# Adding a row shift on VectorE instead of TensorE, and loading the kept token rows in place

## The chip, the cores and the metric

The kernel runs on one core of one Trainium2 chip. A core has five engines that work side by side: TensorE (PE; its weight loads are PEld), VectorE (DVE), ScalarE (ACT), GpSimd (POOL) and SyncE (SP), which here only issues DMAs. The metric is the device time of one launch in microseconds (us). The profile is one execution recorded by the hardware profiler.

## The reference: what is computed

One block with adaptive layer norm: a long convolution (S4 form), then a bilinear GLU, on one sequence of 2048 tokens with 640 features, all in float32.

```python
mod = silu(c) @ w_mod                      # six vectors of 640: sa, ca, ga, sb, cb, gb
h = layernorm(x) * (1 + ca) + sa
# K[d, l] = Re sum_n C[d,n] * exp(dt*A[d,n]*l) * dt*B[d,n],  N = 192
x = x + ga * (causal_conv(h, K) + h * Dskip)
h = layernorm(x) * (1 + cb) + sb
x = x + gb * (((h @ w_gate) * (h @ w_up)) @ w_down)
```

## The kernel before, in words

The program has two halves. The first makes the convolution and writes the new rows x to `x2d` in HBM; the second is the GLU, nearly all matmuls. The features are cut into five column groups of 128 (`db`), the rows into four blocks of 4 x 128 (`q` or `c`).

The first half runs a loop of 120 steps (L1354): 40 units n of three steps each. In them ScalarE makes sines and cosines (`trig`), GpSimd the exponentials (`outer`), VectorE their products (`PtA`, `QtA`, `PtB`, `QtB`: L784, L785, L790, L810) and TensorE sums them to the convolution's kernel (`kg`: L825, L840). Between these, other units are placed by hand: every unit is a generator whose pieces have due numbers in the table `SCHED`, and `due` (L1289) runs the pieces of a step in order of their numbers. A step has 20 numbers; the loop over n ends at 2400, the first half at 2880. Every engine works its instructions in exactly that order, and so does the DMA queue of SP. Which of two or three buffers a unit takes is written out in the strings of `SLOT`.

The units that matter here:

- `u_pre(db, q)`, 20 of them: loads four blocks of normalised rows (L874) and makes the first stage of a transform over the rows: four 64 x 64 matmuls (L886, tile positions in the four quarters of the array), two into each of two PSUM banks `r[0]` and `r[1]`. The shift `sa` is the same for all rows of a column, and so its transform is a constant pattern times a row: four matmuls with a contraction of one row (`t_one` by `shr`) add it. ScalarE copies both banks out (`act`, L235 is the helper's line) and SP stores them to `FH` (L894, L897). For `db` = 0 GpSimd scales the rows first (L878).
- `u_k`, `u_g`, `u_c`: transform of the kernel, second stage of the rows (L907), product of the two (L946 to L956) and the first inverse stage (L967), whose result `W` is stored to `WD` (L972). For the last column group `u_c` works in two parts of 64 columns. The last four `W` stores alternate between two tiles, Wb and Wa.
- `u_d(db, c)`: loads a part of `WD` (`Vt`, L980) and the input rows (`xs`, L982, a ring of two tiles), makes the last inverse stage (L988), adds the input rows (L995) and stores the sum to `x2d` (L996). For the last two column groups and c = 0 or 1 the sum goes into the tile `XB[c]` instead (L992) and is stored from there, since the second half starts with these token rows. The other three column groups of `XB` are loaded back from `x2d` (`rows`, L1384).
- `u_head`: statistics of the rows in `XB` (L1156), the second layer norm, transposes (L1186) and the first GLU matmuls (L1223). While it waits, `warm` (L1196) runs matmuls whose result isn't used.

`need` checks in Python that a unit is placed behind those that it depends on; the waits in the program come from the tile framework. From step 121 on no kernel generation is left. `XB` is made there, in memory that the generation used before.

Of the kernel before, what the change touches and what calls it, by code (L numbers as in the profile page):

```python
# [10 lines left out]
F32 = mybir.dt.float32  # L11
# [7 lines left out]
P = 128  # L19
# [12 lines left out]
    ml=(47, -888, -934),  # L32
    mr=(((138, 140), (110, 111)), ((2, 74), (4, 83)), ((0, 27), (-862, 18))),
    st=(
        (48, 91),
        (69, 100),
        (71, 101),
        (-948, 5),
        (-1006, 0),
        (-965, 89),  # L40
        (-1010, -969),
        (-868, 34),
        (-938, -874),
        (-918, 0),
        (-1003, -929),
        (-947, -909),
        (-919, -868),
        (34, 63),
        (37, 69),
        (-912, 0),  # L50
    ),
    hm=(
        (10, 220),
        (302, 416),
        (-1002, 172),
        (-999, 389),
        (-1010, 182),
        (-961, 147),
        (59, 100),
        (123, 173),  # L60
        (246, 310),
        (290, 372),
        (162, 252),
        (121, 180),
        (210, 293),
        (297, 381),
        (391, 486),
        (473, 556),
    ),
    rstd=(124, 87),  # L70
    tab=(367, 828),
    fo=(162, 162, 208, 238),
    e0=(4, 158),
    ds=(483, 468, 275, 262),
    mc=((87, 192, 194, 200, 210), (153, 286, 303, 326, 337), (270, 359, 369)),
    q=(
# [4 lines left out]
    ),  # L81
    pre=(
# [5 lines left out]
    ),  # L88
    c=(
# [4 lines left out]
        (  # L94
            (2433, 2608, 2608, 2648, 2679, 2703),
            (2425, 2484, 2537, 2554, 2645, 2677),
            (2477, 2493, 2636, 2656, 2680, 2719),
            (2387, 2439, 2532, 2545, 2620, 2633),
# [8 lines left out]
    ),  # L107
    k=(
        (392, 464),
        (371, 384),  # L110
        (474, 512),
        (494, 503),
        (622, 637),
        (592, 599),
        (710, 710),
        (607, 639),
        (640, 677),
        (652, 660),
        (831, 865),
        (797, 803),  # L120
        (973, 990),
        (941, 961),
        (1060, 1060),
        (1060, 1060),
        (1125, 1152),
        (1353, 1363),
        (1274, 1275),
        (1390, 1425),
        (1482, 1495),
        (1506, 1519),  # L130
        (1576, 1590),
        (1524, 1542),
        (1757, 1758),
        (1791, 1791),
        (1747, 1747),
        (1720, 1720),
        (2005, 2019),
        (1893, 1909),
        (2048, 2049),
        (2020, 2031),  # L140
        (2083, 2095),
        (2218, 2252),
        (2287, 2298),
        (2350, 2355),
        (2328, 2328),
        (2344, 2352),
        (2461, 2497),
        (2497, 2510),
    ),
    low=(168, 419, 677, 899, 1101, 1385, 1631, 1857, 2075),  # L150
    w=(2478, 2613, 2684, 2668, 2879, 2879),
    wl=(2590, 2441),
    wm=(2732, 2755),
    h=(2709, 2738, 2775, 2811, 2843, 2843, 2857, 2875),
    g=(
# [1736 lines left out]
```

## Time and profile before

| | us |
|---|---|
| median of three runs | 965.52 |
| lowest and highest | 962.56, 967.35 |
| the profiled execution | 962.34 |
| its span, first to last instruction | 960.6 |
| TensorE busy | 892.6 |
| VectorE busy | 705.6 |
| ScalarE busy | 580.5 |
| GpSimd busy | 471.2 |
| first half, until about | 500 |

The granted TensorE clock is 0.989 on average. A row of the instruction views has start, length in us (or count and lengths in ns), engine, line, operation, output and inputs with shapes; a bracket at its end gives how long the engine idled before it and what ended that. In a group row, `x6 | 3.5, 590` is count, busy us in all, mean ns of one. SPq and ACTq are the queues' DMA issues; what lands later isn't in their length. Busy matmul records overlap, so a full PE isn't a PE at its peak.

### The profile page before, as it was taken

How to read it: one execution, taken by the hardware profiler on the slowest of the kernel's cores; microseconds unless marked ns; L12 is line 12 of the kernel's file. 1: busy time of each engine (PE TensorE's matmuls, PEld its weight loads, DVE VectorE, ACT ScalarE, POOL GpSimd, SP SyncE). 2: the span in 40 equal slices, each digit the busy share in tenths (PEclk: the TensorE clock that was granted, in tenths of full speed). 3: DMA queues.
4: the chain of work that ended last, by engine and by line, in shares of the span. 5: the costliest groups of instructions: out<-in, count | busy, mean ns of one | idle time of the engine just before them, and what ended most of it. 6: DMA issues, size and time to landing. Idle time of an engine off the chain costs nothing.

```text
span 960.6 us, 27559 instructions
## 1 busy us (share of the span) xinstructions
PE 892.6 (93%) x11646; PEld 734.0 (76%) x11646; DVE 705.6 (73%) x1250; ACT 580.5 (60%) x1016; POOL 471.2 (49%) x369
## 2 busy tenths in 40 slices
PE   1898787999899899998889999999999999999998
PEld 1675555878776677887558888889999788888997
DVE  8977888878888986767688555557585766569952
ACT  6989999887988977763276333234463543435430
POOL 3998997986699668750041345320013323231110
PEclk9989999999999999999999999999999999999999
DMA  7876546435267646547894675435536576758875
GB/s 238 324 243 242 186 131 199 146 108 153 78 207 197 187 124 194 184 128 228 277 308 152 192 246 192 165 140 172 200 120 196 171 238 208 244 172 289 253 231 189
DMA packets 158819, 188.59 MB, mean 196 GB/s; under 512 B 9828, under 2 KB 128360, under 8 KB 157544
## 3 DMA queue, kind: packets, MB, share of 16 engines
q1 hardware_dynamic: 149480, 155.51, 50.3%
q0 software_dynamic: 4752, 21.63, 7.8%
q10 hardware_dynamic: 4464, 9.70, 2.7%
q8 instruction: 91, 1.49, 0.6%
q14 instruction: 32, 0.26, 0.1%
HBM read 124.22 MB, written 62.59 MB: 194 GB/s over the span
## 4 chain that ended last, share of the span: by engine, by line
PE 61%; ACT 12%; issue 10%; DVE 7%; POOL 5%; DMA 4%; SPq 0%; POOLq 0%; DVEq 0%; ACTq 0%
PE pa L1095 19%; PE psg L1095 9%; PE pa L1527 7%; PE kg L825 3%; PE kg L840 2%; PE psfa L907 2%; PE psfb L967 2%; PE psfb L907 2%; ACT L235 2%; PE psfc L967 1%; PE psfc L907 1%; PE psfa L967 1%; PE psfc L886 1%; ACT trb L235 1%; ACT tra L235 1%
## 5 line engine op out<-in xcount | busy, mean ns | idle before, releaser
L1072 POOL TENSOR_TENSOR tf<-wur,wgb 128x256 f32<-128x256 f32 x23 | 17.5, 760 | 241.5 <-DVE wtl L1043 193.2
L729 POOL TENSOR_TENSOR EQ<-LQ,RH 128x1536 f32<-128x1536 f32 x40 | 114.8, 2870 | 5.3 <-DVE QtB L785 5.3
L1043 DVE TENSOR_TENSOR wtl<-tf,wth 128x256 fp32r<-128x256 f32 (+1 forms) x72 | 37.0, 516 | 59.2 <-ACT wth L235 59.2
L729 POOL TENSOR_TENSOR Phb<-LH,DH 128x1536 int32<-128x1536 int32 x21 | 60.3, 2871 | 32.6 <-ACT trb L235 19.3
L729 POOL TENSOR_TENSOR EP<-LP,RH 128x768 f32<-128x768 f32 x40 | 61.9, 1547 | 1.7 <-ACT RH L235 1.7
L729 POOL TENSOR_TENSOR Pha<-LH,DH 128x1536 int32<-128x1536 int32 (+1 forms) x20 | 54.1, 2703 | 9.2 <-ACT trb L235 8.5
L1527 PE MATMUL pa<-wsg,sh 128*128 128x384 f32 (+1 forms) x304 | 58.1, 309 | 0.0
L840 PEld LDWEIGHTS kg<-QtB,PtB 64*32 64x32 f32 x2560 | 38.3, 108 | 13.4 <-issue 6.9
L1043 DVE TENSOR_TENSOR wsg<-wga,wsg 128x640 fp32r<-128x640 f32 x36 | 35.5, 988 | 14.8 <-ACT wsg L235 14.8
L840 PE MATMUL kg<-QtB,PtB 64*32 64x64 f32 x2560 | 44.6, 219 | 1.8 <-DVE QtB L785 1.8
L1527 PEld LDWEIGHTS pa<-wsg,sh 128*128 128x128 f32 x304 | 45.4, 188 | 0.0
L1566 POOL DMA_DIRECT2D wsg<-wdc x21 | 11.2, 532 | 66.6 <-PE pa L1579 35.7
L235 ACT ACTIVATE sh<-a 128x512 fp32r<-128x512 f32 x55 | 33.3, 626 | 13.9 <-PE psg L1579 6.2
L1043 DVE TENSOR_TENSOR sl<-a,sh 128x512 fp32r<-128x512 f32 x55 | 38.0, 710 | 3.9 <-ACT sh L235 3.9
L235 ACT ACTIVATE wsg<-wga 128x640 fp32r<-128x640 f32 x36 | 26.2, 731 | 23.7 <-PE pa L1527 12.6
L1095 PE MATMUL pa<-hh,wsg 128*128 128x512 f32 x150 | 40.0, 393 | 0.0
L235 ACT ACTIVATE a<-pa 128x512 f32<-128x512 f32 x12 | 7.2, 596 | 49.9 <-PE pa L1095 49.9
L235 ACT ACTIVATE s<-pa 128x512 f32<-128x512 f32 x12 | 7.2, 598 | 49.2 <-PE pa L1095 47.0
L235 ACT ACT_TABLE_LOAD x25 | 32.1, 1283 | 7.2 <-DMA pta<-A_A_re 4.2
L784 DVE TENSOR_TENSOR QtA<-trb,EQ 128x1024 f32<-128x1024 f32 x22 | 26.8, 1216 | 11.9 <-POOL EQ L729 4.4
L235 ACT ACTIVATE wth<-tf 128x256 fp32r<-128x256 f32 (+1 forms) x72 | 32.4, 481 | 4.5 <-DVE tf L1073 1.8
L1527 PE MATMUL pa<-wsg,sl 128*128 128x384 f32 (+1 forms) x152 | 34.5, 308 | 0.0
(672 smaller groups left out, 3230.0 us busy)
## 6 DMA issues: line engine op xcount, KB each, us to landing
wsg<-wdc POOLq DMA_DIRECT2D x21, 640.0 KB, 5.1
wgb<-B_w_gate SPq DMA_DIRECT2D x24, 320.0 KB, 4.1
wur<-B_w_up SPq DMA_DIRECT2D x24, 320.0 KB, 5.6
wsd<-wsg SPq DMA_DIRECT2D x12, 640.0 KB, 3.7
wga<-wdg SPq DMA_DIRECT2D x12, 640.0 KB, 3.9
wsg<-wsd POOLq DMA_DIRECT2D x12, 640.0 KB, 4.8
wdc<-xb SPq DMA_DIRECT2D x21, 320.0 KB, 4.5
TVb<-WD SPq DMA_DIRECT2D x26, 256.0 KB, 3.5
```

Source lines behind the costliest of these rows:

```text
L235: return S.activation(o, i, f, **kw)
L729: G.tensor_tensor(o.rearrange("p x (h l) -> p x h l", l=8), lo.unsqueeze(2).to_broadcast([P, rows, nh, 8]), hi.unsqueeze(3).to_broadcast([ ...
L784: return [lambda: V.tensor_tensor(Qt[:, :, :, 0:32], tr[:, :, :, ::-1], e[:, :, 0:32].unsqueeze(1).to_broadcast([P, 2, R, 32]), op=OP.mult ...
L825: PE.matmul(kg[j * 32 : j * 32 + 32, dd, :], PtA[:, c, dl * 4 + j, :], QtA[:, c, dl * 4 + j, :], start=dd == 0 and c == 0, stop=False, til ...
L840: PE.matmul(kg[j * 32 : j * 32 + 32, dd, :], PtB[lo : lo + 64, c, r, :], QtB[lo : lo + 64, c, r, :], start=False, stop=dd == 7 and c == 1, ...
L907: PE.matmul(r[c][par * 64 : par * 64 + 64, i, :], t_tw[:, k0 + k, c, :], src[:, k, :], start=True, stop=True, tile_position=(0, par * 64))
L967: PE.matmul(r[par][:, i], t_ti[lo : lo + 64, qd * 4 + i, c, :], y[lo : lo + 64, i, :], start=k == 0, stop=k == len(x) - 1, tile_position=( ...
L1043: V.tensor_tensor(lo, v, hi, op=OP.subtract)
L1072: E.tensor_tensor(t[:, 0:2], u[:, 0:2], g[:, 0:2], op=OP.subtract)
L1095: PE.matmul(ps, w[a][:, k], x[b][:, l], start=first and n == 0 and m == 0, stop=n == 2 and m == len(ks) - 1, skip_group_check=True)
L1527: PE.matmul(AC[tb][t][c], x[:, ts], w[:, cs], start=st, stop=f == NF - 1 and n == 2 and (c == 0 or t % 2 == 1))
L1566: G.dma_start(WD[q], wdc[:, q // 3, q % 3])
```

## The change

There are three edits, and an order that was written anew:

1. In `u_pre` the one-row matmuls are left for bank 1 only. Bank 0's shift is added as VectorE takes that bank out of PSUM: `scalar_tensor_tensor` with the shift row (spread over the partitions in `shr`), a column of constants `t_on`, and `r[0]`. Bank 1 is still copied by ScalarE. The table `t_c` shrinks from 800 to 737 columns accordingly.
2. In `u_d`, the kept rows (`db` = 3 or 4, c = 0 or 1) no longer load their input rows into the ring `xs`. A new `kept_l` loads both column groups at once into `XB[c]`, and the sum is made in place.
3. The kept rows are stored once for both column groups, after the second of them is done.
4. Nearly every due number in `SCHED` and every string in `SLOT` is another (`xs` has 16 entries instead of 20). The numbers of the units named above and in the prediction are shown for both; in `d`, rows 4 and 5 are column groups 3 and 4, and each entry holds the numbers of the loads, the matmuls and the add.

```diff
 SCHED = dict(
...
     d=(
...
-        ((2440, 2500, 2511), (2392, 2442, 2445), (2656, 2725, 2725), (2657, 2687, 2687)),
-        ((2736, 2744, 2754), (2780, 2829, 2831), (2836, 2874, 2875), (2749, 2762, 2784)),
+        ((2410, 2495, 2559), (2408, 2438, 2661), (2692, 2692, 2730), (2651, 2688, 2715)),
+        ((2734, 2749, 2787), (2799, 2838, 2843), (2848, 2876, 2878), (2746, 2756, 2813)),
     ),
...
-    wl=(2590, 2441),
-    wm=(2732, 2755),
-    h=(2709, 2738, 2775, 2811, 2843, 2843, 2857, 2875),
+    wl=(2602, 2481),
+    wm=(2735, 2751),
+    h=(2562, 2755, 2793, 2818, 2854, 2858, 2862, 2876),
...
+    xl=(2441, 2442),
...
     one = np.tile(f.sum(1).reshape(1, 2, 1, 32), (128, 1, 2, 1))
+    ones = np.tile(f.sum(1).T, (4, 1))
...
-    ct = kconst.tile([P, 800], F32, name="ct")
+    ct = kconst.tile([P, 737], F32, name="ct")
...
-    t_one = ct[:, 384:512].rearrange("p (c m) -> p c m", c=2)
+    t_one = ct[:, 384:448]
+    t_on = ct[:, 448:449]
...
-                for c in range(2):
+                for c in range(2) if i == 0 else (1,):
                     o = 64 * (j ^ c)
-                    PE.matmul(r[c][o : o + 64], (t_s1h, t_one)[i][a, c], h[a] if i == 0 else shr[a, d0].unsqueeze(1).to_broadcast([1, 4, P]),
-                              start=i == 0, stop=i == 1, tile_position=(64 * j, o))
+                    PE.matmul(r[c][o : o + 64], t_s1h[a, c] if i == 0 else t_one[a], h[a] if i == 0 else shr[a, d0].unsqueeze(1).to_broadcast([1, 4, P]),
+                              start=i == 0, stop=i == 1 or c == 0, tile_position=(64 * j, o))
         yield
         for c in range(2):
             Ft = ring(fp, [P, 4, P], "hf")
-            act(Ft, r[c])
+            if c == 0:
+                V.scalar_tensor_tensor(Ft, shr[:, d0].unsqueeze(1).to_broadcast([P, 4, P]), t_on, r[c], op0=OP.mult, op1=OP.add)
+            else:
+                act(Ft, r[c])
...
-        xs = ring(fp, [P, 4, P], "xs")
-        SY.dma_start(xs, xin[:, 4 * c : 4 * c + 4, db * P : db * P + P])
+        d0 = slice(db * P, db * P + P)
+        kept = db >= NB - 2 and c < 2
+        if not kept:
+            xs = ring(fp, [P, 4, P], "xs")
+            SY.dma_start(xs, xin[:, 4 * c : 4 * c + 4, d0])
         yield
...
         mark("d", c)
-        if db >= NB - 2 and c < 2:
-            V.tensor_tensor(XB[c][:, :, d0], ps, xs, op=OP.add)
+        if kept:
+            need(1, "xl", c)
             xs = XB[c][:, :, d0]
-        else:
-            V.tensor_tensor(xs, ps, xs, op=OP.add)
+        V.tensor_tensor(xs, ps, xs, op=OP.add)
+        if kept:
+            mark("kept", c)
+            if done["kept", c] < 2:
+                return
+            d0, xs = LAST, XB[c][:, :, LAST]
         SY.dma_start(x2d[:, 4 * c : 4 * c + 4, d0], xs)
...
+    LAST = slice((NB - 2) * P, NB * P)
...
+            def kept_l(tb):
+                SY.dma_start(XB[tb][:, :, LAST], xin[:, 4 * tb : 4 * tb + 4, LAST])
+                mark("xl", tb)
+
             for j in range(2):
                 XB[j] = mk(f"xb{j}", [P, 4, D])
+                at(T0["xl"][j : j + 1], once(kept_l), j)
                 at(T0["wl"][j : j + 1], once(rows), j)
```

More of the change, by code (lines that the diff above doesn't have):

```diff
@@ L70 @@
[L70 to L75, printed above, removed]
-    q=(
[4 rows of a table removed]
+    ml=(38, 14, -923),
+    mr=(((103, 138), (85, 117)), ((35, 82), (23, 45)), ((-877, 33), (0, 56))),
+    st=(
+        (60, 115),
+        (40, 121),
+        (69, 127),
+        (-999, 8),
+        (-984, 3),
+        (-998, 109),
+        (-1010, -963),
+        (17, 37),
+        (-986, -888),
+        (1, 3),
+        (-998, -939),
+        (-983, -907),
+        (-883, 1),
+        (23, 67),
+        (36, 68),
+        (5, 5),
+    ),
@@ new lines @@
+    hm=(
+        (-889, 197),
+        (121, 398),
+        (-1010, 305),
+        (85, 399),
+        (-1010, 176),
+        (-1007, 270),
+        (77, 140),
+        (217, 273),
+        (39, 136),
+        (171, 232),
+        (172, 227),
+        (134, 181),
+        (294, 470),
+        (331, 369),
+        (402, 469),
+        (251, 445),
+    ),
+    rstd=(142, 86),
+    tab=(553, 739),
+    fo=(149, 149, 202, 228),
+    e0=(1, 159),
+    ds=(339, 378, 319, 440),
+    mc=((120, 175, 197, 201, 209), (192, 273, 273, 309, 317), (264, 369, 392)),
@@ L81 @@
+    q=(
[4 rows of a table added]
     ),
     pre=(
[5 rows of a table removed]
-    ),
-    c=(
[4 rows of a table removed]
-        (
[L95 to L98, printed above, removed]
[5 rows of a table added]
+    ),
+    c=(
[4 rows of a table added]
+        (
+            (2380, 2593, 2606, 2606, 2655, 2720),
+            (2446, 2513, 2534, 2567, 2634, 2656),
+            (2455, 2551, 2627, 2642, 2651, 2697),
+            (2431, 2453, 2513, 2566, 2623, 2623),
         ),
@@ L150 @@
-    low=(168, 419, 677, 899, 1101, 1385, 1631, 1857, 2075),
-    w=(2478, 2613, 2684, 2668, 2879, 2879),
-    wl=(2590, 2441),
-    wm=(2732, 2755),
-    h=(2709, 2738, 2775, 2811, 2843, 2843, 2857, 2875),
-    g=(
[5 rows of a table removed]
[5 rows of a table added]
+    ),
+    k=(
+        (402, 407),
+        (224, 230),
+        (454, 556),
+        (421, 426),
+        (484, 507),
+        (517, 548),
+        (639, 657),
+        (603, 603),
+        (706, 716),
+        (664, 680),
+        (777, 781),
+        (803, 804),
+        (1006, 1012),
+        (1029, 1037),
+        (1046, 1059),
+        (1046, 1075),
+        (1295, 1322),
+        (1120, 1137),
+        (1252, 1252),
+        (1388, 1406),
+        (1410, 1420),
+        (1505, 1522),
+        (1556, 1567),
+        (1481, 1509),
+        (1808, 1839),
+        (1737, 1774),
+        (1753, 1756),
+        (1784, 1785),
+        (1840, 1856),
+        (1883, 1912),
+        (1996, 2008),
+        (2063, 2073),
+        (2085, 2096),
+        (2141, 2191),
+        (2362, 2374),
+        (2274, 2274),
+        (2321, 2321),
+        (2447, 2455),
+        (2494, 2510),
+        (2452, 2466),
+    ),
@@ L161 @@
+    low=(167, 428, 668, 910, 1139, 1389, 1628, 1864, 2075),
+    w=(2473, 2612, 2690, 2703, 2759, 2879),
+    wl=(2602, 2481),
+    wm=(2735, 2751),
+    h=(2562, 2755, 2793, 2818, 2854, 2858, 2862, 2876),
+    g=(
[5 rows of a table added]
     ),
+    xl=(2441, 2442),
 )
 SLOT = dict(
-    Kt="abababbaabababbababa",
-    Ph="ababababababababababbbabababababaaababbb",
-    PtA="abababababababababababababababbabaababba",
-    TV="baabababaabbaabbbabbaababbaababbaabbabbaababab",
-    W="abbbbbabababbbbabbaabbaba",
-    f16="abababa",
@@ L177 @@
-    "a",
-    xs="aabababbabaaabababab",
+    Kt="ababababababbabbaaba",
+    Ph="abababababababababababababababababababbb",
+    PtA="babaababababababababababababababaaababab",
+    TV="ababababaabababbaabbababbaaabbabbbbabaabababab",
+    W="baaabbaaabbabaabaaabbbaba",
+    f16="abababa",
+    gh="bacbabcbcabacbacacbbabcabcabacbacabcabc",
+    hf="cbabcbabcacbaabccbcbaccbcababcacbccabaababcacbbaaaccabccbabaabbaa",
+    psf="bacbaacbaacccabbcabcbacbbbcabcbcaabacabbbcbcbcabcaaacbbcbcabcababccabcabcacbacbbabacbacabcbabacbabcabcbbacbacbacbaccacba"
@@ L179 @@
+    "bacbcbcaabccbaaacbaccacabbccabacbacbabccabaacbcacbccbacabcaacbbacbacbaccaacbacbbababacbacbabcbabacbacbabcabacbacabcabcba"
+    "baabcababcbacbacbcbacbacbacacacbcabc",
+    tr="ababababababababababababababababababababababababababbabbababababababababababababababababababababbbabbabbababaabbabaababa"
+    "b",
+    xs="aabababbaabbaaab",
 )
@@ L224, in _tables @@
     t = {"t_tw": tw.reshape(128, 4096), "t_ti": ti.reshape(128, 4096),
-         "t_c": np.concatenate([perm, s1h.reshape(128, 128), one.reshape(128, 128), s1k.reshape(128, 256), ib.reshape(128, 32)], 1)}
+         "t_c": np.concatenate([perm, s1h.reshape(128, 128), one[:, 1].reshape(128, 64), ones[:, 0 : 1], s1k.reshape(128, 256), ib.reshape(128, 32)], 1)}
     return {k: np.ascontiguousarray(v, dtype=np.float32) for k, v in t.items()}
@@ L303, in tile_kernel @@
     WQ = (SY, S)
-    ct = kconst.tile([P, 800], F32, name="ct")
+    ct = kconst.tile([P, 737], F32, name="ct")
     perm = ct[:, 0:256]
     t_s1h = ct[:, 256:384].rearrange("p (c m) -> p c m", c=2)
-    t_one = ct[:, 384:512].rearrange("p (c m) -> p c m", c=2)
-    t_s1k = ct[:, 512:768].rearrange("p (c k j) -> p c k j", c=2, j=4)
-    t_ib = ct[:, 768:800]
+    t_one = ct[:, 384:448]
+    t_on = ct[:, 448:449]
+    t_s1k = ct[:, 449:705].rearrange("p (c k j) -> p c k j", c=2, j=4)
+    t_ib = ct[:, 705:737]
     shr = kconst.tile([P, D], F32, name="shr")
```

81 lines of the change are left out of this document (removed), and 42 rows, old and new, of tables (c, d, g, pre).

## The prediction

> **What bounds the kernel now.** I read the page first (busy shares, the chain that ended last), then the busy time by stage, then the instructions in order of time around the two places that the change touches.
>
> ```profile
> PE 892.6 (93%) x11646; PEld 734.0 (76%) x11646; DVE 705.6 (73%) x1250; ACT 580.5 (60%) x1016; POOL 471.2 (49%) x369
> ...
> PE 61%; ACT 12%; issue 10%; DVE 7%; POOL 5%; DMA 4%; SPq 0%; POOLq 0%; DVEq 0%; ACTq 0%
> ```
>
> TensorE is busy for 93% of the span and holds 61% of the chain. That is a mean over stages, so the next view cuts the span at the places where the work changes. Its columns are the stretch, its length, busy time of PE, PEld, DVE, ACT and POOL with instruction counts, the granted clock, the share of the DMA engines and GB/s.
>
> ```profile
> 24.00:96.00 72.00, 63.26 (x912) 47.46 (x912) 61.22 (x122) 65.59 (x102) 65.31 (x46) 0.93 0.77 270
> 96.00:168.00 72.00, 57.86 (x1408) 39.51 (x1410) 60.69 (x86) 69.32 (x118) 63.27 (x37) 0.95 0.55 172
> 168.00:432.00 264.00, 251.81 (x6090) 199.29 (x6088) 213.53 (x288) 215.45 (x369) 207.48 (x114) 0.99 0.52 155
> 432.00:500.00 68.00, 59.22 (x819) 42.12 (x815) 49.01 (x129) 26.91 (x50) 9.78 (x15) 1.00 0.86 267
> 500.00:960.60 460.60, 455.72 (x2404) 402.41 (x2402) 300.70 (x545) 188.87 (x362) 116.43 (x138) 1.00 0.61 200
> ```
>
> From 500 us on TensorE idles for 4.9 of 460.6 us, and the change leaves that half of the program alone. The change works in the first four rows. From 96 to 168 us ScalarE is the full engine (idle 2.7 of 72 us) while TensorE idles 14.1 and VectorE 11.3. From 168 to 432 us TensorE is the bound (idle 12.2 of 264), with VectorE idle for 50.5 and ScalarE for 48.5. From 432 to 500 us nothing is full: that stage runs on waits.
>
> **The removed matmuls.** Each of the 20 row units (u_pre, five column groups by four) ends with four matmuls of one row each that add the shift, two per output bank; the change keeps the two of bank c = 1. The next view is TensorE in order of time (start, length in us).
>
> ```profile
> 145.23 0.64 PE L886 MATMUL psfb<-shr,ct 1*64 1x512 f32 x1
> ...
> 145.25 0.64 PE L886 MATMUL psfc<-shr,ct 1*64 1x512 f32 x1
> 145.71 0.59 PE L886 MATMUL psfb<-shr,ct 1*64 1x512 f32 x1
> ...
> 145.73 0.59 PE L886 MATMUL psfc<-shr,ct 1*64 1x512 f32 x1
> 146.28 0.43 PE L840 MATMUL kg<-QtB,PtB 64*32 64x64 f32 x16
> ```
>
> The four lie in the four quarters of the array and run side by side: four records start within 0.02 us, their second passes 0.48 us later, and the whole group takes 145.23 to 146.28, about 1.0 us. The two that stay still need both passes, one after the other in the same quarter. So 40 removed matmuls, 80 records, shorten TensorE by nothing unless the next group fits into the two empty quarters. I take 0; the other end is half a group each time, 20 x 0.5 = 10 us. [...]
>
> **The copies.** Bank c = 0 is no longer copied out by ScalarE but by VectorE's scalar_tensor_tensor, which adds shift times column constant on the way. The first two rows are instruction groups of ScalarE's old copy and of a VectorE instruction of the same kind and size with one operand in PSUM; the next three say who waits today for the row units' matmuls (us, times); the last three count the one-row matmuls from 96 to 168 us.
>
> ```profile
> L235 ACT ACTIVATE hfa<-psfc 128x512 f32<-128x512 f32 x6 | 3.5, 590 | 4.2 <-PE psfa L886 2.9 <-PE psfb L886 1.3
> ```
>
> ```profile
> L948 DVE SCALAR_TENSOR_TENSOR ghb<-psfb,ghb x4: 691/692/693, 158.3 to 411.2; 128x512 f32<-128x512 f32 x4
> ```
>
> ```profile
>   ACT hfa L235: 8.7, 6
>   ACT hfc L235: 2.0, 3
>   ACT hfb L235: 1.1, 2
> ```
>
> ```profile
> L886 PE MATMUL psfc<-shr,ct x20: 587/613/638, 101.8 to 145.7; 1*64 1x512 f32 x20
> ...
> L886 PE MATMUL psfb<-shr,ct x20: 587/612/638, 116.9 to 167.0; 1*64 1x512 f32 x20
> ...
> L886 PE MATMUL psfa<-shr,ct x16: 587/612/638, 101.8 to 167.0; 1*64 1x512 f32 x16
> ```
>
> ScalarE loses 20 x 0.59 = 11.8 us, VectorE gains 20 x 0.69 = 13.8. Of the 20 units, 56 / 8 = 7 lie between 96 and 168 us, where ScalarE is full: 4.1 us come off it there, 4.8 go to a VectorE that idles 11.3. The other 13 units give ScalarE 7.7 and cost VectorE 9.0 of its idle 50.5 us, under a TensorE that sets the pace. The best end is -4.1 us, if ScalarE alone sets the pace of that stretch. The worst end is the wait: ScalarE stands 11.8 us in 11 waits for these matmuls, and on VectorE the products for the kernel generation (QtA, PtA, QtB) are queued behind the new copy, for which the next matmuls wait. Against that, bank 0 is now complete before the one-row group, 1.0 us sooner, which takes 11 x 1.0 off and leaves 0.8. So -4.1 to +11.8; the other engines of that stretch (POOL idle 8.7) would soon hold a freed ScalarE, so I take -1.
>
> **The end of the first half, 432 to 500 us.** The kept rows of the last two column groups (c = 0 and 1) lose their ring tiles: two loads of 512 KB go straight into XB, two stores of 512 KB replace four of 256 KB. The bytes are the same; two issues are saved on each side. The rows are in order of time (start, length, engine; in brackets the idle time before and what ended it), then two steps of the chain.
>
> ```profile
> 440.50 0.69 DVE L992 TENSOR_TENSOR xb<-psfa,xsa 128x512 f32<-128x512 f32 x1 [3.52 <-PE psfa L988]
> 441.69 0.45 SPq L1384 DMA_DIRECT2D xb<-x2d  x1
> ...
> 446.56 0.68 DVE L992 TENSOR_TENSOR xb<-psfa,xsa 128x512 f32<-128x512 f32 x1
> ...
> 460.40 0.33 ACTq L972 DMA_DIRECT2D WD<-Wa  x1
> 466.55 0.60 ACT L235 ACTIVATE Wa<-psfb 128x512 f32<-128x512 f32 x1 [3.47 <-DMA WD<-Wa]
> 467.67 0.33 ACTq L972 DMA_DIRECT2D WD<-Wa  x1
> ```
>
> ```profile
> 469.39 0.69 DVE L995 TENSOR_TENSOR xsa<-psfc,xsa 128x512 f32<-128x512 f32 x1 [7.01 <-DMA xsa<-A_u]
> ...
> 470.59 6.27 DVE L1156 BATCH_NORM_STATS2 a<-xb 128x6 f32<-128x128 f32 x32
> ...
> 472.14 0.91 SPq L980 DMA_DIRECT2D TVb<-WD  x2
> 474.75 0.37 SPq L982 DMA_DIRECT2D xsb<-A_u  x1
> ...
> 476.12 1.32 PE L988 MATMUL psfa<-TVb,ct 64*32 64x512 f32 x8
> ...
> 477.80 0.69 DVE L992 TENSOR_TENSOR xb<-psfa,xsb 128x512 f32<-128x512 f32 x1 [0.94 <-DMA xsb<-A_u]
> ```
>
> ```profile
> 470.70 4.03 DMA x2d<-xsb
> 474.75 2.96 DMA xsb<-A_u
> ```
>
> The chain runs through a store that frees ring tile xsb (4.03) and the load into it (2.96), to the add at 477.80. Take both away and the add waits for its matmuls instead, which end at 476.12 + 1.32 = 477.44: 0.4 us sooner, no more. Those hang on the last store of W (467.67), held 3.47 us by the store before it on the same tile. The wait of 7.01 us at 469.39 is for rows that are *not* kept (column group 3, c = 2 or 3); it stays a ring load, issued at about the same place (2651 and 2692 against 2656 and 2657 in the order), and VectorE stood in front of the 6.27 us of statistics because of it. If that load comes early enough, since 1 MB of loads now goes out near 441 us, the whole 7.0 go. The other way: the two early loads are due at 2441, where XB is free, so near 441.7; the first kept add is due at 2559, about where the second of today's two stands (446.56). With twice the bytes of the transfer that took 4.03 us it would land at 441.7 + 8.1 = 449.8 and hold VectorE for 3.2 us, with five product groups of the last column group queued behind the add. Moving the second kept add to 2661 takes the 3.52 us wait at 440.50 off VectorE. So -7.0 to +3.2. I take -2, nearer to the 0.4 that the matmuls leave than to the 7.0, since the ring load keeps its place.
>
> **The new order.** Nearly all due numbers change; the same units move by some tens of steps. Their number and the loop under them stay. What a different order can do I bound by the dips of the granted clock, in three of the stretches (clock is the third number from the end):
>
> ```profile
> 54.00:60.00 6.00, 6.00 (x82) 5.51 (x82) 3.17 (x18) 5.94 (x9) 5.92 (x6) 0.50 0.81 243
> 84.00:90.00 6.00, 3.29 (x8) 2.15 (x9) 5.93 (x11) 5.92 (x8) 5.31 (x3) 0.79 0.65 224
> ...
> 318.00:324.00 6.00, 4.41 (x88) 2.69 (x88) 6.00 (x12) 5.92 (x8) 2.39 (x1) 0.72 0.52 151
> ```
>
> They lose 6 x 0.50, 6 x 0.21 and 6 x 0.28 = 6.0 us of clock. An order that feeds TensorE evenly has none of them, one that starves it as often again has three more: -6 to +6, and 0 taken, since the diff shows no direction. [...]
>
> **The sum.** 0 - 1 - 2 + 0 = -3 us. The profiled execution took 962.34 us with a span of 960.6; so 959.3. The median of the three runs, 965.52, lies 3.2 above the profiled execution; the same distance gives **962.5 us**. About 0.5% (4.8 us) is what a measurement of this kernel can tell from no change.
>
> **The rivals.**
> 1. *ScalarE's stretch and the ring wait both give way*: -4.1 for the seven copies, -7.0 for the load at 469.39: 951.2 profiled, 954.4 as a median. For it: ScalarE's 2.7 us idle of 72, and a DMA share of 0.86 at the end of the half that the early loads relieve. Against it: POOL is nearly as full as ScalarE, and the ring load keeps its place.
> 2. *The emptied quarters are filled*, so TensorE does gain half a group each time: -10 and the other terms, 949.3 profiled, 952.5. For it only that TensorE is the bound from 168 to 432; against it the four simultaneous starts.
> 3. *VectorE comes to the new copy before the matmuls are done*, as ScalarE does today: all 11.8 us of waiting then stand on VectorE, nothing of the relief of ScalarE is left, and the end of the half still gives its 2: +9.8, 972.1 profiled, 975.3 as a median. It decides from the point where the copies' time and waits in the stretch from 96 to 168 us exceed VectorE's idle 11.3; the stretch's seven units bring 4.8 of work, so 6.5 us of waits in it are enough. With half of the waits it gives +3.9, 969.4. For it: TensorE already waits for VectorE's products (us, times, longest).
>
> ```profile
> PE kg L825 <- DVE PtAb L790: 4.6, 3, 2.0
> ```
>
> Against it: the bank is complete 1.0 us sooner.
> 4. *The change does not do what it says at the end of the half*: the add is held by its matmuls (477.44) anyway, and only 0.4 us come of it; with 0 elsewhere 961.9 profiled, 965.1.
>
> **How the numbers follow.** The forecast has 0.30 and rival 4 has 0.08; both are within 0.5%, so 0.38 for the same. Rival 1 has 0.29 and rival 2 has 0.08: 0.37 faster. Rival 3 has 0.25, all of it slower. The forecast's own range is 957.7 to 967. The stated range goes from 951, just under rivals 1 and 2, to 974, between rival 3's half and its whole; some 0.1 is left out on either side.
>
> **What the profile after would show.** TensorE: 80 fewer records of the one-row matmuls and nearly the same idle time from 168 to 432 us; a clear drop there would be rival 2. ScalarE about 12 us less, VectorE about 14 us more busy. VectorE's wait for the row units' matmuls: under 3 us bears me out, over 6 is rival 3. In the stretch from 96 to 168 us, less length for the same work is rival 1. At the end of the first half, no ring load ahead of the first add of column group 4; the add held by its matmuls; the wait at the group 3 ring load still several us. The second half must be as long as before. I am wrong in the mechanism if the first matmul of the second half moves by over 5 us while none of these waits moved.

## The result, and the profile after

The changed kernel takes 970.47 us (median of 20 runs, 965.77 to 975.67), the kernel before 963.37 on the same chips (20 runs, 959.05 to 967.44). The ratio is 1.0075, with a 95% interval of 1.0059 to 1.0090: 7.1 us slower. The profiled execution of after took 966.46 us with a span of 964.6, so the pair of profiles shows 4.1 of the 7.1 us; the profile of after lies 4.0 below its median, the one of before 1.0 below its own.

The page of after, busy times and chain:

```profile
PE 897.4 (93%) x11566; PEld 737.1 (76%) x11566; DVE 716.3 (74%) x1270; ACT 572.1 (59%) x996; POOL 471.1 (49%) x369
...
PE 70%; ACT 5%; DVE 5%; DMA 2%; issue 2%; POOL 0%; DVEq 0%; SPq 0%; POOLq 0%
```

TensorE has 80 records fewer and is busy 4.8 us longer, VectorE 10.7 longer with 20 instructions more, ScalarE 8.4 shorter with 20 fewer. TensorE is not idle longer: 964.6 - 897.4 = 67.2 us against 960.6 - 892.6 = 68.0. The 4.0 us between the two spans stand in TensorE's busy time, with fewer records. The stretches of after, with the columns of the prediction's view:

```profile
24.00:96.00 72.00, 62.60 (x925) 46.28 (x924) 61.63 (x124) 66.03 (x105) 66.94 (x49) 0.91 0.74 249
96.00:168.00 72.00, 61.06 (x1393) 40.95 (x1395) 63.95 (x92) 64.92 (x108) 62.02 (x36) 0.93 0.60 193
168.00:432.00 264.00, 247.53 (x5906) 196.22 (x5899) 219.32 (x299) 205.76 (x349) 206.82 (x114) 0.98 0.52 152
432.00:500.00 68.00, 59.86 (x921) 44.19 (x914) 48.20 (x128) 27.21 (x51) 7.62 (x13) 1.00 0.80 251
500.00:964.60 464.60, 459.30 (x2425) 404.86 (x2423) 302.60 (x549) 191.98 (x367) 119.29 (x142) 1.00 0.62 202
```

From 96 to 168 us ScalarE has given up 4.4 us (69.32 to 64.92), as the change meant. From 168 to 432 us TensorE, which sets the pace there, idles 16.5 us instead of 12.2 and gets 184 records fewer done, of which 52 are removed ones. The last group of the kernel generation, before and after, comes 3.5 us later, so most of the pair's loss lies ahead of it:

```profile
436.32 1.10 PE L840 MATMUL kg<-QtB,PtB 64*32 64x64 f32 x64
```

```profile
439.80 1.21 PE L843 MATMUL kg<-QtB,PtB 64*32 64x64 f32 x64
```

The mean granted clock is 0.982 in this profile and 0.989 in the one of before. The clock records of the two traces have 34.1 us at half the clock against 20.5 (the last 25 us left out), 13.6 us more. The pair overstates this somewhat: 0.989 is the highest mean clock among 78 executions of the kernel before, whose median is 0.9825; over 20 executions of the changed kernel the median is 0.9785. The rows of TensorE in time order, where it stands longest in this stretch:

```profile
313.18 0.98 PE L843 MATMUL kg<-QtB,PtB 64*32 64x64 f32 x54
317.01 0.38 PE L843 MATMUL kg<-QtB,PtB 64*32 64x64 f32 x10 [2.85 <-issue]
324.32 1.98 PE L865 MATMUL psfa<-ct,Ktb 128*64 128x128 f32 x16 [3.71 <-DVE RH L609]
```

A group of 64 matmuls stops after 54 of them, for 2.85 us, and for nothing that the profile shows ("issue"). VectorE's table for the next seeds comes late behind it, TensorE waits another 3.71 us for the bank, and then 16 matmuls take 1.98 us. Sixteen of the same kind in the kernel before, and the stretch of after with its granted clock (third from the end):

```profile
442.15 1.04 PE L862 MATMUL psfa<-ct,Kta 128*64 128x128 f32 x16
```

```profile
320.00:326.00 6.00, 2.29 (x20) 1.60 (x16) 5.90 (x12) 5.76 (x8) 2.00 (x1) 0.50 0.52 138
```

With 0.50 of the clock granted the 16 took 1.98 us, with 1.00 (432 to 500 us, a row of the prediction) 1.04. This place isn't lost as a whole: the kernel before stands 2.55 us at nearly the same time, ahead of another group and also for "issue", and its clock dips there as well (0.72 from 318 to 324 us, a row of the prediction).

```profile
319.59 1.93 PE L988 MATMUL psfb<-TVb,ct 64*32 64x512 f32 x8 [2.55 <-issue]
```

Who waited for the row units' matmuls (us, times), and one group of the new copies:

```profile
  ACT hfb L237: 9.6, 7
  ACT hfa L237: 2.7, 3
  DVE hfa L895: 2.4, 3
  ACT hfc L237: 1.7, 2
```

```profile
L895 DVE SCALAR_TENSOR_TENSOR hfb<-shr,ct,psfc 128x512 f32<-128x512 f32 x4 | 3.0, 738 | 0.0
```

VectorE waits 2.4 us for these matmuls. ScalarE waits 14.0 us for the other bank, more than the 11.8 for both before. A copy takes 0.74 us where I had put 0.69. The end of the first half, VectorE's rows in time order:

```profile
451.28 0.68 DVE L1002 TENSOR_TENSOR xb<-psfc,xb 128x512 f32<-128x512 f32 x1
464.49 0.68 DVE L1002 TENSOR_TENSOR xb<-psfa,xb 128x512 f32<-128x512 f32 x1
470.54 0.69 DVE L1002 TENSOR_TENSOR xsb<-psfb,xsb 128x512 f32<-128x512 f32 x1 [0.68 <-PE psfb L996]
...
472.00 6.28 DVE L1169 BATCH_NORM_STATS2 a<-xb 128x6 f32<-128x128 f32 x32
482.02 0.69 DVE L1002 TENSOR_TENSOR xb<-psfc,xb 128x512 f32<-128x512 f32 x1 [3.02 <-PE psfc L996]
```

The kept adds of group 3 wait for nothing, and the 7.01 us wait for the ring load is gone. The first add of group 4 is held by its matmuls instead, 3.02 us, and comes at 482.02 where it came at 477.80. It is 4.2 us late, of which 3.5 were lost before the end of the generation, and the program behind it is as late: the second half is as long as before (TensorE idle 5.3 of it, 4.9 before).

### The profile page after: what moved, and what is told of

Same layout as the page of the kernel before. It is cut to its first block, busy times and chain, and to the rows that moved or that the text cites. A ratio compares the mean times of both kernels' runs of the same rounds, so it can differ in the third digit from the quotient of the medians.

```text
span 964.6 us, 27405 instructions
## 1 busy us (share of the span) xinstructions
PE 897.4 (93%) x11566; PEld 737.1 (76%) x11566; DVE 716.3 (74%) x1270; ACT 572.1 (59%) x996; POOL 471.1 (49%) x369
## 4 chain that ended last, share of the span: by engine, by line
PE 70%; ACT 5%; DVE 5%; DMA 2%; issue 2%; POOL 0%; DVEq 0%; SPq 0%; POOLq 0%
PE pa L1108 20%; PE psg L1108 10%; PE pa L1545 7%; PE pa L1597 6%; PE kg L843 3%; PE psfc L973 3%; PE psfb L913 2%; PE kg L828 2%; PE psfb L973 2%; PE psfa L913 2%; PE psfc L913 2%; PE psg L1597 2%; PE psfc L889 1%; PE psfa L973 1%; PE psfb L889 1%
## 5 line engine op out<-in xcount | busy, mean ns | idle before, releaser
L732 POOL TENSOR_TENSOR EQ<-LQ,RH 128x1536 f32<-128x1536 f32 x40 | 114.7, 2867 | 10.7 <-DVE QtB L788 10.7
L1056 DVE TENSOR_TENSOR wsg<-wga,wsg 128x640 fp32r<-128x640 f32 x36 | 33.0, 918 | 17.0 <-ACT wsg L237 17.0
L237 ACT ACTIVATE wsg<-wga 128x640 fp32r<-128x640 f32 x36 | 26.3, 730 | 25.3 <-PE pa L1545 12.8
```

The lines of the kernel that those rows point to most:

```text
L237: return S.activation(o, i, f, **kw)
L732: G.tensor_tensor(o.rearrange("p x (h l) -> p x h l", l=8), lo.unsqueeze(2).to_broadcast([P, rows, nh, 8]), hi.unsqueeze(3).to_broadcast([ ...
L1056: V.tensor_tensor(lo, v, hi, op=OP.subtract)
```

## The experiments

Each kernel was timed beside the kernel before, whose medians lay between 963.2 and 963.8; of each there are 4 to 12 runs (20 of the changed kernel) and one profile.

| | order | copies of first banks | kept loads | us | ratio (95%) |
|---|---|---|---|---|---|
| e1 | old | VectorE, 20 | no | 988.74 | 1.0275 (1.0242 to 1.0308) |
| e13 | old | VectorE 8, ScalarE 12 | no | 966.36 | 1.0037 (1.0019 to 1.0055) |
| e14 | old | VectorE 12, ScalarE 8 | no | 992.62 | 1.0298 (1.0270 to 1.0325) |
| e15 | old | ScalarE; 20 idle VectorE instructions | no | 964.86 | 1.0025 (1.0007 to 1.0043) |
| e2 | old | ScalarE | yes | 970.60 | 1.0085 (1.0063 to 1.0108) |
| e16 | old | ScalarE | yes, add later | 971.35 | 1.0077 (1.0055 to 1.0100) |
| e17 | old | ScalarE | yes, bank held | 966.97 | 1.0047 (1.0029 to 1.0064) |
| e4 | new | ScalarE | yes | 976.40 | 1.0146 (1.0118 to 1.0175) |
| e5 | new | VectorE, 20 | no | 971.88 | 1.0108 (1.0073 to 1.0142) |
| e6 | new | VectorE, 20, one-row matmuls back | yes | 972.66 | 1.0099 (1.0068 to 1.0130) |
| after | new | VectorE, 20 | yes | 970.47 | 1.0075 (1.0059 to 1.0090) |
| e7 | new, loads spread | VectorE, 20 | yes | 966.85 | 1.0036 (1.0017 to 1.0056) |
| e19 | new, one load later | VectorE, 20 | yes | 968.83 | 1.0057 (1.0035 to 1.0079) |
| e9 | as e7, one step later | VectorE, 20 | yes | 968.71 | 1.0059 (1.0036 to 1.0082) |
| e18 | new, records moved | VectorE, 20 | yes | 969.03 | 1.0064 (1.0041 to 1.0088) |
| e20 | as e7, records moved | VectorE, 20 | yes | 969.80 | 1.0072 (1.0050 to 1.0094) |

### The parts one by one

**VectorE's copies alone.** The first edit in the old order: VectorE copies all first banks, 40 one-row matmuls go.

```diff
-            act(Ft, r[c])
+            if c == 0:
+                V.scalar_tensor_tensor(Ft, shr[:, d0].unsqueeze(1).to_broadcast([P, 4, P]), t_on, r[c], op0=OP.mult, op1=OP.add)
+            else:
+                act(Ft, r[c])
```

> The kernel before with the first edit alone: VectorE copies the first bank of every row unit, the one-row matmuls write the second bank only; due numbers and ring tiles as before, no kept loads. Theory A (the new order costs the time: the transfers of several units go out together and TensorE's instructions come late behind them): within 3 us of the kernel before. Theory B (VectorE's copies cost it): 5 to 9 us slower than the kernel before, with waits of TensorE for VectorE's products up by several us. Theory C (the kept loads and the single store at the end of the first half cost it): within 3 us of the kernel before.

Measured: 25.3 us slower, far over any theory's number. Waits of TensorE in this kernel (us, times, longest), the largest three of ten that sum to 19.3 us; then the place of the second of them, VectorE and TensorE in time order:

```profile
PE psfc L912 <- DVE hfb L894: 5.3, 2, 2.8
PE psfb L972 <- DVE hfa L894: 3.6, 1, 3.6
PE psfa L972 <- DVE hfa L894: 2.2, 1, 2.2
```

```profile
314.51 0.59 PE L888 MATMUL psfb<-hfb,ct 64*64 64x512 f32 x1
...
320.13 0.42 PE L972 MATMUL psfb<-TVa,t_ti 64*128 64x128 f32 x1 [3.61 <-DVE hfa L894]
```

```profile
317.08 1.21 DVE L786 TENSOR_TENSOR QtA<-tra,EQ 128x1024 f32<-128x1024 f32 x1
318.21 1.21 DVE L787 TENSOR_TENSOR QtA<-tra,EQ 128x1024 f32<-128x1024 f32 x1
319.34 0.74 DVE L894 SCALAR_TENSOR_TENSOR hfa<-shr,ct,psfb 128x512 f32<-128x512 f32 x1
```

Bank psfb is complete at 314.51 + 0.59 = 315.10. VectorE is behind with its products and copies it at 319.34, 4.2 us later; TensorE's next group wants this bank and stands. So VectorE does not wait for TensorE here (rival 3), and no wait of VectorE for a row unit's matmuls is in the whole trace of e1: TensorE waits for VectorE. In the changed kernel one such wait is left:

```profile
PE psfb L865 <- DVE hfb L895: 0.6, 1, 0.6
```

The next three runs test this reading, two with a dose and one with the time alone.

**Eight copies, the twelve others.** Only the units named in `ON_V` are copied by VectorE. The first run has the eight whose copy came within 1 us of the matmuls in e1, the second the other twelve; all one-row matmuls stay in both.

```diff
+            if c == 0 and (db, q) in ON_V:
+                V.scalar_tensor_tensor(Ft, shr[:, d0].unsqueeze(1).to_broadcast([P, 4, P]), mults[:, 3:4], r[c], op0=OP.mult, op1=OP.add)
+            else:
+                act(Ft, r[c])
```

> The kernel before with 8 of the 20 first banks copied by VectorE, those that VectorE copied within 1 us of their matmuls when all 20 were moved in the old order; all one-row matmuls stay and VectorE multiplies its row by zero. If the 25 us come from banks that VectorE frees late (waits of TensorE for these copies, 19.3 us with all 20), within 4 us of the kernel before and under 3 us of such waits. If they come from VectorE's own time (0.74 us a copy), 8 of 20 of it: about 10 us slower.

> The kernel before with the other 12 first banks copied by VectorE, those that it copied 1 us or more behind their matmuls when all 20 were moved in the old order; one-row matmuls stay, VectorE multiplies its row by zero. If the price hangs on banks that VectorE frees late: 15 to 25 us slower than the kernel before, with 12 us or more of TensorE's waits for these copies. If it hangs on VectorE's time alone: 12 of 20, about 15 us, or, going by the eight copies' 2.9 us, 4 to 5 us.

Measured: eight cost 2.9 us, with two waits of TensorE for them (1.0 us); twelve cost 28.8 us, all of the 25.3 and more, and over the 15 to 25 that I had expected, with nine entries that sum to 19.5 us, the largest:

```profile
PE psfc L911 <- DVE hfb L893: 5.4, 2, 2.9
PE psfb L971 <- DVE hfa L893: 3.6, 1, 3.6
```

**The time of the copies without a bank behind it.**

```diff
             act(Ft, r[c])
+            if c == 0:
+                V.bn_stats(rv[:, 0:6], shr[:, 0:512])
```

> The kernel before, all copies by ScalarE, and behind each first copy a VectorE instruction that nobody waits for and that waits for nobody (statistics over 512 elements of a constant row, some 0.75 us by the 478 ns of 320 elements, results not used): VectorE's time of the 20 copies without a bank behind it. If VectorE's time costs the 25 us of the copies in the old order: 15 us or more slower than the kernel before. If the late banks cost them: within 5 us of it.

Measured: 1.1 us slower. The group of the added instructions (count, busy us, mean ns):

```profile
L893 DVE BATCH_NORM_STATS2 rv<-shr 128x6 f32<-128x512 f32 x20 | 13.7, 684 | 0.0
```

VectorE took 13.7 us more work at the same places in its order and the kernel lost 1.1. The price of the copies in the old order is that they come late, and not VectorE's time. Theory B, as far as it speaks of time, falls. TensorE's waits for the full banks are 19.3 of the 25.3 us. What else a late copy holds up, no run separates: from 70 to 440 us SP's queue stands 105.9 us for the stores behind these copies in e1, and 82.2 us for the same stores in the kernel before.

**The kept loads in the old order.** Edits 2 and 3 alone. The three runs differ in when the first two kept units have their matmuls and adds.

```diff
-        ((2440, 2500, 2511), (2392, 2442, 2445), ...
+        ((2440, 2500, 2511), (2392, 2476, 2483), ...    # e2
+        ((2440, 2500, 2520), (2392, 2476, 2519), ...    # e16
+        ((2440, 2500, 2520), (2392, 2442, 2519), ...    # e17
```

> The kernel before with the kept loads and the single store alone; old order but for one unit, whose matmuls go from 2442 to 2476 and whose add goes from 2445 to 2483, so that the add does not stand directly behind its load. Copies by ScalarE. My step 3 said -2 us (-7.0 to +3.2); the run without the kept loads lost 1.4 us against the changed kernel, so here 1 to 3 us faster than the kernel before. If the loads come late for the add (landing near 450 us), 1 to 3 us slower instead.

> The run with the kept loads in the old order, and the two first kept adds moved behind two steps of VectorE's products (due 2483 to 2519 and 2511 to 2520; one of TensorE's banks changes letter for it). Its predecessor had VectorE stand 10.6 us at the first add for a load that was issued only 8.5 us before. If that wait is the whole price of the kept loads in the old order (7.2 us), it falls below 4 us here and the kernel comes to 961 to 966 us, as fast as before or a little faster; if the price lies elsewhere (the loads crowd others), it stays at 968 us or more.

> The kept loads in the old order once more, now with the unit's matmuls back at 2442, so that its ring tile comes free as before, and the add at 2519; one TensorE bank is held from 2442 to 2519 for it. Before, VectorE stood 10.6 us for the load, then, with the matmuls moved, 6.7 us for the ring tile. If such a wait on VectorE is the whole price, none over 3 us is left between 436 and 460 us and the kernel comes within 3 us of the kernel before or below it; if the held bank or the crowded transfers take over, it stays 5 us or more slower.

Measured: 7.2, 7.6 and 3.8 us slower, where I had put 1 to 3 us faster or slower for e2. The load's issue on SP's queue and VectorE's add in e2, VectorE's wait in e16, and the adds in e17:

```profile
439.30 0.50 SPq L1393 DMA_DIRECT2D xb<-A_u  x1
```

```profile
447.80 0.69 DVE L995 TENSOR_TENSOR xb<-psfc,xb 128x512 f32<-128x512 f32 x1 [10.59 <-DMA xb<-A_u]
```

```profile
447.55 0.69 DVE L945 TENSOR_TENSOR TVa<-psfb,ghb 128x512 f32<-128x512 f32 x1 [6.70 <-PE psfc L989]
```

```profile
446.06 0.69 DVE L995 TENSOR_TENSOR xb<-psfa,xb 128x512 f32<-128x512 f32 x1
...
471.55 0.69 DVE L995 TENSOR_TENSOR xsa<-psfc,xsa 128x512 f32<-128x512 f32 x1 [6.27 <-DMA xsa<-A_u]
```

In e2 the load takes 447.80 - 439.30 = 8.5 us and VectorE stands 10.59 us for it. In e16 the add doesn't wait, but the unit's matmuls, moved behind, hold the ring tile TVa, and VectorE stands 6.70 us for that: my expectation had overlooked it. In e17 neither is left; a wait of 3.7 us for another load and the held bank remain, and so does the wait for group 3's ring load, 6.27 us of the 7.01; the 3.8 us lie between the two answers that I had set. The kept loads by themselves are no gain in the old order in any of the three.

**The new order without the kept loads.** Ring tiles and single stores again; `xs` has 20 entries.

```diff
-        kept = db >= NB - 2 and c < 2
-        if not kept:
-            xs = ring(fp, [P, 4, P], "xs")
-            SY.dma_start(xs, xin[:, 4 * c : 4 * c + 4, d0])
+        xs = ring(fp, [P, 4, P], "xs")
+        SY.dma_start(xs, xin[:, 4 * c : 4 * c + 4, db * P : db * P + P])
```

> The changed kernel without the kept loads: the input rows of the last two column groups go through the ring tiles again and each unit stores its own rows; the new order and VectorE's copies stay. Theory A: 5 to 9 us slower than the kernel before. Theory B: the same 5 to 9 us slower. Theory C: within 3 us of the kernel before. My own step for the end of the first half (-2 us for the kept loads) would make it 2 us slower than the changed kernel.

Measured: 971.88, 1.4 us over the changed kernel, with intervals that overlap. The loss is not in the kept loads (theory C falls). From e1 to here only the order changes (due numbers and ring letters): 988.74 - 971.88 = 16.9 us are what the new order gives back.

**The new order with ScalarE's copies.**

```diff
-                for c in range(2) if i == 0 else (1,):
+                for c in range(2):
...
-            if c == 0:
-                V.scalar_tensor_tensor(...)
-            else:
-                act(Ft, r[c])
+            act(Ft, r[c])
```

> The changed kernel with all copies back on ScalarE and all 80 one-row matmuls; new order and kept loads stay. Two row units (second and third of the third column group in the order) copy straight behind their matmuls, since ScalarE would otherwise stand in front of a bank that it has to free itself. Theory A (the new order's own clusters of work and transfers cost the time): 3 to 10 us slower than the kernel before, as the changed kernel is. Theory D (the order was only made for VectorE's copies, whose price in the old order was 25 us, and is no better or worse by itself): slower than the changed kernel by over 5 us, because ScalarE's 12 us and the late banks come back in an order that doesn't expect them. Theory B (VectorE's copies cost the 7 us also in the new order): within 3 us of the kernel before.

Measured: 13.0 us slower than the kernel before and 5.9 slower than the changed kernel, as theory D has it (its 5 us). In the new order the copies on VectorE are a gain of 5.9 us; without them this order is the worst of the new ones. e2 has the same edits in the old order, so the new order costs 976.40 - 970.60 = 5.8 us here. Two units' copies were moved for this run, so the 5.9 are rough.

**The one-row matmuls back.**

```diff
-                for c in range(2) if i == 0 else (1,):
+                for c in range(2):
...
-                V.scalar_tensor_tensor(Ft, ..., t_on, r[c], ...)
+                V.scalar_tensor_tensor(Ft, ..., mults[:, 3:4], r[c], ...)
```

> The changed kernel with the 40 one-row matmuls of the first bank back; VectorE's instruction stays and multiplies the row by zero, so that its time stays. The row is now added by TensorE as in the kernel before. If these matmuls cost nothing (my step 1), within 2 us of the changed kernel; if they cost half a group each, 10 us slower than it. Under theory A a shift of TensorE's instructions by 80 may move the place where they come late, so some us in either direction, with the stall near 314 us gone or moved.

Measured: 972.66, 2.2 us over the changed kernel, with overlapping intervals. Half a group each time, 10 us, is excluded.

### The stall near 314 us

Queue q8 carries packets of the kind "instruction", and by their count I take them for TensorE's. The queue's row on the page of after, and the rows of two stretches around the stall (packets, MB, share of the DMA engines); in the first stretch the queue has no row:

```profile
q8 instruction: 91, 1.49, 0.7%
```

```profile
DMA packets 2241, 1.96 MB, mean 216 GB/s; under 512 B 93, under 2 KB 2000, under 8 KB 2241
...
q1 hardware_dynamic: 2241, 1.96, 70.3%
```

```profile
q1 hardware_dynamic: 123, 0.08, 100.6%
q8 instruction: 1, 0.02, 23.3%
```

91 packets for 11566 matmuls and as many weight loads are 254 records each. Between 305.4 and 314.5 us not one started, while 1.96 MB of data went through; the next starts between 314.50 and 314.75, inside the stall. That made theory A concrete, and the next runs test it: SP's queue had stood 4.3 us for one of VectorE's new copies, which it stores, then 2.6 us in front of a load that waits for its ring tile, and then sent several transfers together.

**The loads spread.** One load is put ahead of the waiting one, the waiting one behind three stores.

```diff
     g=(
...
-        ((1664, 1807, 1807), ...
+        ((1650, 1807, 1807), ...
     d=(
...
-        ..., (1656, 1742, 1747)),
+        ..., (1690, 1742, 1747)),
```

> The changed kernel with two due numbers changed: the FH load of the third column group's first unit goes from 1664 to 1650, the WD and input loads of one unit of the second group from 1656 to 1690, so that SP's queue no longer stands in front of the load that waits for a ring tile and then sends 2.3 MB at once. Theory A: TensorE's stall of 2.85 us near 314 us and the 10.2 us of half clock behind it go, 3 to 5 us faster than the changed kernel. Theories B and C: within 1.5 us of the changed kernel.

Measured: 966.85, 3.6 us faster than the changed kernel, 3.4 over the kernel before. The group now runs through and the clock from 320 to 326 us is 0.78; the wait for the seeds' bank stays:

```profile
314.75 1.39 PE L843 MATMUL kg<-QtB,PtB 64*32 64x64 f32 x64
...
323.07 1.35 PE L865 MATMUL psfa<-ct,Ktb 128*64 128x128 f32 x12 [4.57 <-DVE RH L609]
```

**Only the later load; the waiting step behind the next group.** e19 has the second of the two numbers alone. e9 has both and moves the step that waits 4.57 us (1737 to 1740).

> The changed kernel with one of the two due numbers of the spread loads: the WD and input loads of one unit of the second column group go from 1656 to 1690, the FH load stays at 1664. SP's queue then no longer stands in front of the load that waits for its ring tile. If that queue is what cost the 3.6 us, 965.5 to 968 us, with no stall of TensorE over 1 us near 314; if the earlier FH load brought it, within 1.5 us of the changed kernel (970.5).

> The changed kernel with the spread loads, and one more due number: the products' last step that waits 4.6 us for a bank which VectorE's table frees (due 1737) goes to 1740, behind the next group of matmuls, which has its operands. If TensorE's order decides this stretch, 1 to 3 us faster than with the spread loads alone (964 to 966 us) and the kernel before is reached; if VectorE's chain of tables decides it, within 1 us of it, with the wait of 4.6 us moved to the next group.

Measured: e19 968.83, between the two answers; it doesn't tell which half of the spread brings what. e9 968.71: no gain over 966.85, so putting the group first does not help. That VectorE's chain of tables decides that stretch instead isn't shown: I had expected within 1 us and the wait of 4.6 moved on, and there are 1.9 us and a wait of 3.54 at the same place.

**The records moved.** 16 tiny matmuls ahead of the first ones, at 1.2 us, where TensorE is idle (in e18 for 1.20 us before them and 4.12 behind); in e18 on the changed kernel, in e20 on the spread loads.

```diff
         def trans(src, o):
+            for _ in range(16 if db == 0 and src is rho else 0):
+                PE.matmul(o[0:11, 0, 0:1], mults, mults[:, 0:1], start=True, stop=True)
```

> The changed kernel with 16 matmuls of 11x1 ahead of the first ones, whose bank they share; nothing else moves. They add 64 records (a load and a matmul, twice each) to TensorE's program near 12 us, where it is idle. Theory A (TensorE stalls where its program runs out: at records that lie 256 apart, 11457 in the changed kernel, when a piece of program is late): the stall near 314 us comes 64 records earlier in the program, after some 22 instead of 54 of the 64 matmuls of the products' group, and all such stalls are at records of the same remainder by 256; time within 3 us of the changed kernel. If the stall belongs to the work at that place (an operand, a bank), it stays after 54 of 64.

> The changed kernel with the spread loads and with the 64 records of the small matmuls at the start. If TensorE running out of program at a burst is what the spread took away, the moved records take away nothing more: 966 to 968 us, as with the spread alone. If the place of the records decides by itself where such stalls fall, it differs from the spread alone by 2 us or more, up or down, with other stalls over 1 us at records of one remainder by 256.

Measured: e18 969.03, e20 969.80. In e18 the group runs through, so the stall did not belong to the work at that place; but it didn't come 64 records earlier either. In e20 a new stall stands elsewhere, TensorE's rows of e18 and then of e20:

```profile
318.00 1.10 PE L845 MATMUL kg<-QtB,PtB 64*32 64x64 f32 x64
```

```profile
125.40 0.28 PE L834 MATMUL kg<-dskt,ident 128*128 128x8 f32 x1
128.81 0.17 PE L834 MATMUL kg<-dskt,ident 128*128 128x8 f32 x1 [3.13 <-issue]
```

Counting TensorE's records by start (weight loads and matmuls, with the semaphore and drain records between them) shows where such stalls lie. The stall at 314 us is ahead of record 11457, the one of e20 ahead of record 3265; both leave 193 when divided by 256. Gaps of over 0.38 us between 70 and 500 us, ahead of a record with this remainder, one profile each:

```
                          gaps, sum in us          records of the largest
before                     1      1.28             16577
old order: e1, e13, e14, e15, e2, e16, e17
                          1 to 2  0.63 to 2.54
after                      7      8.24             11457 (2.85), 1729 (2.21)
e5  no kept loads         10      9.70             11457 (2.80)
e9, e20, e19, e7          3 to 6  5.42, 4.23, 4.05, 3.61
e4, e6, e18               2 to 3  3.84, 2.93, 2.63  7873 (2.47, 2.30, 1.80)
```

In the changed kernel 7 of 34 gaps of that length have the one remainder of 256, in the kernel before 1 of 35. The packets speak for instructions that come late at these places: in the 17 profiles there are 55 gaps with this remainder, and every one ends 1.22 to 1.58 us behind the end of an instruction packet; of the 532 other gaps 32 do. That TensorE has run out of instructions there is my estimate from these counts; the profile names nothing that it waits for.

The sum is 7.0 us larger in after than in before, more than the 4.1 us between these two profiles. It is not the whole cause: e18 has 2.63 us of it and is still 5.9 us slower than the kernel before; e6 has 2.93 and is 9.2 slower. Nor is the stall at record 11457 shown to be worth the 3.6 us of e7: e18 and e19 don't have it either and are only 1.4 and 1.6 us faster than the changed kernel.

## Why the prediction was wrong

Forecast were -3 us, which I counted as no change (962.5 us); measured are +7.1. The range (951 to 974) held the time, but not the direction. By its steps:

1. **The removed matmuls (0).** Held, as far as a run can tell: 80 records fewer, TensorE no less busy, e6 within its uncertainty. Rival 2 is out.
2. **The copies (-1, between -4.1 and +11.8).** Wrong in what it looked at. I priced the time on both engines and the wait of the copying engine for the matmuls, and found 0.74 for 0.69 us and 2.4 us of waits, under my mark of 3. Who waits for the bank *behind* the copy was in no bound. In the old order that is 19.3 us of TensorE's waits and +25.3 us; the time itself is worth 1.1.
3. **The end of the first half (-2, between -7.0 and +3.2).** In the new order the kept loads are worth 1.4 us, with an interval that reaches none (e5); in the old order they cost 3.8 to 7.6, outside my bounds. I let the wait for group 3's ring load stay; it went from 7.01 to 0.68. No gain of that size is seen, since the first add of group 4 then waits for its matmuls, as I had said (3.02 us). The other end, VectorE standing for the kept load, is real: 10.59 us in e2, where the add stands soon behind the load.
4. **The new order (0, between -6 and +6).** This is the step that failed. I took it as a term of its own, without direction, and put the dips of the clock at nothing. The dips came: 13.6 us more at half the clock in the pair of profiles are, counted as the prediction counts them, 6.8 us, just over its upper bound. The loss of the pair stands in TensorE's busy time and not in its waits: it is busy 4.8 us longer and idle 0.8 us shorter. All nine kernels of the new order look like this: 34 to 51 us at half the clock (20.5 before), TensorE busy for 897 to 907 us (892.6) and idle for 63 to 71 (68.0). But e15, in the old order, has 34.1 us at half the clock too and a span only 2.3 us longer, so the dips say where the time goes and not why. That a TensorE fed evenly has no dips was my assumption, and no run shows it: in the pair TensorE idles 0.8 us less and has the 13.6 us more at half the clock.

The steps are not separate terms either. The order is worth -16.9 us with VectorE's copies (e1 to e5) and +5.8 with ScalarE's, beside the kept loads (e2 to e4). The copies cost 25.3 us in the old order and gain 5.9 in the new one, the kept loads cost 7.2 (e2) or gain 1.4. The new order is made for the copies: it takes their 19.3 us of waits down to 0.6. Copies and order together, which I had put at -1, came to +8.4 (e5).

Rival 3 came nearest in time (975.3, with half of the waits 969.4) with the wrong mechanism: it decides where VectorE waits for the matmuls, which it hardly does. My last mark (the second half over 5 us late with none of these waits moved) came close, with 4.2 us in the pair of profiles: the loss came before the end of the generation (3.5 us there), and none of the waits that I had marked shows it.

Shown: in the old order the copies cost because they come late, most of it through held banks; the new order gives most of it back; in the new order the kept loads are not the loss; what is left stands, in the profiles, in TensorE's busy time at a lower clock; two due numbers that spread a burst of loads are worth 3.6 us in one comparison. Open: why the new order has more half-clock time. Its gaps at the one remainder of 256 sum to more than those of the old one (2.63 to 9.70 us against 0.63 to 2.54), but why, and how much of the loss comes from them, no run settles. Moving 64 records, which adds only tiny matmuls where TensorE is idle, moved the time by -1.4 us once and by +3.0 the other time, so differences of that size between the new kernels are not to be read as effects of their edits. None of the versions beats the kernel before.

## What to carry to other kernels

When a copy out of PSUM moves to another engine, price the bank and not the instruction (here, in the old order, 25.3 us for the copies against 1.1 for 13.7 us of VectorE's time with no bank behind it): find what stands in that engine's queue ahead of the copy, and which matmuls need the bank next. An order written by hand and the engines it was written for are one term; cost them together, or not at all. Compare the busy and the idle time of the engine that bounds the kernel before you list waits: here the idle time is no longer (67.2 us against 68.0) and the busy time is (897.4 against 892.6). Where TensorE stops inside a group of equal matmuls with nothing named, count its records and look at the instruction queue before looking at operands.

## What the runs showed of the hardware that I had not expected

- TensorE stood 2.85 us inside a group when no instruction packet had started for 9.1 us (305.4 to 314.5) under 70% DMA load; 7 of the 34 gaps of over 0.38 us in the changed kernel lie whole multiples of 256 records apart, and the 55 gaps of this kind in the 17 profiles end 1.22 to 1.58 us behind the end of a packet. The longest was 3.13 us (e20).
- After that stall the granted clock was 0.50 for the 6 us from 320 to 326, and 16 matmuls took 1.98 us instead of 1.04. In the clock records of before and after the stretches at half the clock last 3.41, 6.83 or 10.24 us, but for the last one of each.
- 13.7 us of extra VectorE work in an engine that is busy for 73% of the span cost 1.1 us; 14.8 us (20 x 0.74) of copies at the same places cost 25.3.
- A load of 512 KB took 8.5 us until the waiting add began (439.30 to 447.80); the estimate was 8.1, twice the 4.03 of a transfer of half its size.
